# One order string and four small edits: cheaper FFT angles, an early table switch, a joined load and paired stores in a fused FFT-convolution and FFN kernel

## The chip, the cores and the metric

The kernel runs on one core of one Trainium2 chip. The metric is device microseconds (us) of one execution. Several executions of each kernel are timed beside executions of the kernel before on the same chip, and one of them is profiled. The span of a run is shorter than its device time (189.8 for 191.62). The profile of the kernel before is of a run outside the four of the comparison. Engines: PE is TensorE, ACT ScalarE, DVE VectorE, POOL GpSimd, SP the engine that issues most transfers.

## The reference, cut to what matters

```python
# x: 2048 tokens x 640, bf16; F = 1728
def reference(A_q, A_k, A_v, A_shift_k, A_ssm_k, A_ssm_D, B_x, B_w1, B_b1, B_w2, B_b2):
    x  = A_q
    xn = layernorm(x)                                  # over the 640 columns
    # long convolution:
    kv = causal_conv4(A_k, A_shift_k) * A_v            # 4 taps per column
    y  = irfft(rfft(kv, 4096) * rfft(A_ssm_k, 4096))[:2048]
    s  = xn * (y + kv * A_ssm_D)
    # FFN:
    h  = gelu(xn @ B_w1 + B_b1)
    g  = silu(h @ B_w2 + B_b2)
    return x + s * g
```

## The kernel before

The convolution is done as matrix products in two stages. The first (`s1`) multiplies by a table `W` of sines and cosines, its result is staged in SBUF, stored to DRAM and loaded again in another layout; the second (`s2`) follows, then the product of the two spectra, and the inverse (`i1`, `i2`) with a trip through DRAM between. The two FFN products (`f1` with GELU, `f2` with SiLU) are interleaved with it on PE. The columns are done in two halves, b0 and b1.

The kernel first describes every operation and what it depends on. A long string, `ORDER`, then says in which order the operations are emitted, on which engine, and in which slot of its buffer pool each result lies. That string is the schedule; 800 operations are placed by it.

```python
plan = Plan(unpack(ORDER))
...
# angles: m = tok * k4, an integer, then m mod L and (m + L/4) mod L
op("iq1", "DVE", lambda e: eng(e).tensor_single_scalar(out=m_v, in_=m_v, scalar=L - 1, op=ALU.bitwise_and), writes=[m_b],
   after=[o for o in plan.ops if o.kind == "xn"])
def iq2(e):
    eng(e).tensor_single_scalar(out=a_v, in_=m_v, scalar=L // 4, op=ALU.add)
    eng(e).tensor_single_scalar(out=a_v, in_=a_v, scalar=L - 1, op=ALU.bitwise_and)
...
sc = 2.0 * math.pi / L
op("wsin", "ACT", lambda e: nc.scalar.activation(out=W_c[:, 1, :], in_=m_v, func=ACT.Sin, scale=sc * (1.0 - EPS), bias=bias_pi[:]), ...)
op("wsin", "ACT", lambda e: nc.scalar.activation(out=W_c[:, 0, :], in_=a_v, func=ACT.Sin, scale=-sc * (1.0 - EPS), bias=bias_p[:]), ...)
...
def finish(j):                       # one row tile of 128 tokens
    op("fin", "DVE", lambda e: eng(e).tensor_tensor(out=xs(j), in0=xn[:, j, :], in1=xs(j), op=ALU.add), ...)
    op("store", "SP", lambda e: nc.sync.dma_start(out=out_v[:, j, :], in_=xs(j)), ...)
...
def conv_unit(b, u):                 # second stage of the convolution, unit u of half b
    kin, uin = Buf(pool=kin_pool, parts=nh), Buf(pool=uin_pool, parts=nh)    # four u buffers
    ...
    chain("uin", op("uin", "SP", lambda e: rd(scrU, uin), ...))              # load
    # s2k, s2u on PE, eviction in place, product on DVE, i1 on PE,
    # then the u buffer takes i1's result and is stored before it is loaded anew
```

## Time and profile before

| | before |
|---|---|
| device time, median of 4 runs of the comparison | 190.49 us (189.39 to 191.81) |
| profiled run | 191.62 us, span 189.8, mean granted PE clock 0.976 |
| busy PE / DVE / ACT | 176.4 / 164.6 / 146.5 us |
| ACT table loads | 8, of 1.28 us each |

"Slow" needs a word. On one core the label means only that the run was over 1.5% above the fastest of its kernel. I collected the 56 runs of the kernel before that accompanied four of my batches: they spread from 186.82 to 193.12 us. In 36 of them the mean clock was under 0.99, and they averaged 190.4 us; the other 20 averaged 189.5, and the 11 of these at 0.995 or more 188.9. So some dip of PE's clock comes in most runs of this kernel, not in all, and is worth some 1 to 1.5 us. The mean doesn't say where the clock fell: the profiled run has one dip, near 130 us, but the second profile that I took has two (clock 0.50 from 8 to 10 us, 0.66 from 130 to 135).

The prediction below shows the busy row, the slices, the window rows and the chain at the hole in PE's work. Two more views: the first is ACT's start (start in us, duration, engine, line, operation, what was written and read):

```profile
2.02 1.28 ACT L368 ACT_TABLE_LOAD   x1 [2.02 <-issue]
...
9.53 2.48 ACT L265 COPY xnT<-ps 128x640 bf16<-128x640 bf16 x4
12.03 1.28 ACT L456 ACT_TABLE_LOAD   x1
13.32 1.44 ACT L456 ACTIVATE W<-mm,bias_pi 128x1024 bf16<-128x1024 int32 x1
```

ACT loads a first table, evicts the first transposes, and only at 12.03 loads the table with Sin. W is there at 16. The second is what PE waited for between 28 and 80 us (who waits, for what: us in total, times, longest):

```profile
PE ps L610 <- DVE v_all L639: 0.9, 1, 0.9
PE ps L513 <- ACT sl L580: 0.5, 1, 0.5
PE ps L576 <- ACT sl L580: 0.5, 1, 0.5
PE ps L513 <- ACT hT L519: 0.2, 1, 0.2
```

Four waits, 2.1 us together: these are the "small waits" of the prediction.

### The profile page before, as it was taken

To read this page: it belongs to the slowest core of one execution; us is meant where nothing else is said; L and a number is where in the kernel's file an instruction comes from. 1 tells how busy PE (TensorE), PEld (TensorE's weight loads), DVE (VectorE), ACT (ScalarE), POOL (GpSimd) and SP (SyncE) were. 2 spreads that over 40 slices of the span, in tenths; PEclk is the share of its full clock that TensorE was granted. 3 is DMA by queue.
4 is the path that set the end of the run, shared out by engine and by line. 5 is a ranking of instruction groups with operands and counts; after the bars stand their busy time and mean duration, and the time that the engine had idled before them with its cause. 6 is when DMAs were issued, how large, how long until landed. Compare 5 with 4: busy or idle time off the path is not lost.

```text
span 189.8 us, 4770 instructions
## 1 busy us (share of the span) xinstructions
PE 176.4 (93%) x1907; PEld 92.2 (49%) x1907; DVE 164.6 (87%) x302; ACT 146.5 (77%) x225; POOL 20.6 (11%) x35
## 2 busy tenths in 40 slices
PE   7899999999898899999999999985999999989990
PEld 2285543345554465656433444332246565646660
DVE  6799979994799999999989999996498998669993
ACT  2899799797986999999999999994599987111110
POOL 4470410031021030000001100110010000000000
PEclk9999999999999999999999999996699999999997
DMA  5999969999999987898699998879762999568375
GB/s 141 350 418 414 408 200 348 323 310 379 384 333 328 234 282 206 155 293 252 137 298 286 243 380 256 240 192 327 215 207 50 342 303 337 157 214 338 107 260 191
DMA packets 44410, 51.44 MB, mean 271 GB/s; under 512 B 7442, under 2 KB 38547, under 8 KB 44388
## 3 DMA queue, kind: packets, MB, share of 16 engines
q1 hardware_dynamic: 43216, 47.03, 77.8%
q0 software_dynamic: 1024, 4.10, 6.4%
q8 instruction: 15, 0.25, 0.6%
q14 instruction: 7, 0.06, 0.1%
q10 hardware_dynamic: 148, 0.01, 0.1%
HBM read 31.47 MB, written 18.35 MB: 262 GB/s over the span
## 4 chain that ended last, share of the span: by engine, by line
PE 45%; DMA 29%; DVE 17%; ACT 4%; issue 2%; SPq 1%; POOLq 0%; ACTq 0%; DVEq 0%
PE ps L513 18%; PE ps L576 14%; DMA scrC<-v_all 9%; DMA mm<-scrC 7%; DMA kT<-in_x_dram 4%; PE ps L610 4%; DMA scrK<-mm 3%; PE ps L723 3%; DVE stats L383 3%; DMA v_all<-scrU 3%; DVE xn L784 2%; DMA x<-in_x_dram 2%; ACT mm L265 2%; DVE kT L557 2%; PE ps L777 1%
## 5 line engine op out<-in xcount | busy, mean ns | idle before, releaser
L513 PE MATMUL ps<-xnT,w_sb 128*128 128x512 bf16 (+1 forms) x280 | 64.5, 379 | 0.9 <-ACT sl L580 0.5
L576 PE MATMUL ps<-w_sb,hT 128*128 128x320 bf16 x432 | 63.6, 300 | 0.5 <-ACT sl L580 0.5
L576 PEld LDWEIGHTS <-hT 128*128 128x128 bf16 x448 | 41.8, 98 | 21.6 <-issue 5.8
L265 ACT CAST mm<-ps 128x640 bf16<-128x640 f32 (+1 forms) x62 | 39.4, 703 | 4.4 <-DMA scrK<-mm 3.3
L513 PEld LDWEIGHTS <-w_sb 128*128 128x128 bf16 x280 | 26.6, 101 | 31.4 <-issue 8.9
L265 ACT CAST v_all<-ps 128x960 bf16<-128x960 f32 (+2 forms) x38 | 33.4, 916 | 6.4 <-PE ps L723 4.1
L519 ACT ACTIVATE hT<-ps,b_f 128x512 bf16<-128x512 f32 (+1 forms) x56 | 36.9, 706 | 1.7 <-PE ps L513 1.2
L580 ACT ACTIVATE sl<-ps 128x320 bf16<-128x320 f32 x32 | 13.6, 445 | 21.1 <-PE ps L576 18.8
L784 DVE TENSOR_TENSOR xn<-ps,xn 128x640 bf16<-128x640 f32 x16 | 12.6, 817 | 3.8 <-PE ps L777 3.0
L736 DVE TENSOR_TENSOR kT<-v_all,k_all 128x960 bf16<-128x960 bf16 x16 | 9.8, 652 | 4.2 <-ACT v_all L265 4.2
L723 PEld LDWEIGHTS <-tabs 64*32 64x32 bf16 x704 | 7.6, 92 | 11.7 <-issue 7.3
L635 DVE TENSOR_TENSOR mm<-k_all,mm 128x2560 bf16<-128x2560 bf16 x8 | 11.8, 1480 | 0.1
L632 DVE TENSOR_TENSOR mm<-k_all,mm 128x2560 bf16<-128x2560 bf16 x8 | 11.8, 1478 | 0.0
L723 PE MATMUL ps<-v_all,tabs 64*32 64x240 bf16 (+1 forms) x352 | 9.0, 274 | 2.9 <-DMA v_all<-scrU 2.9
L265 DVE CAST v_all<-ps 128x960 bf16<-128x960 f32 (+1 forms) x8 | 8.6, 1070 | 2.1 <-PE ps L755 1.0
L383 DVE BATCH_NORM_STATS2 stats<-kT 128x6 f32<-128x320 bf16 x16 | 6.9, 472 | 3.8 <-DMA kT<-in_x_dram 3.8
L610 PEld LDWEIGHTS <-W 64*128 64x128 bf16 x128 | 4.5, 94 | 10.7 <-issue 8.0
L736 DVE TENSOR_TENSOR k_all<-v_all,xtra 128x960 bf16<-128x960 bf16 (+1 forms) x16 | 9.0, 609 | 0.1
L390 POOL TENSOR_TENSOR rstd<-veps,mhalf 128x4 f32<-128x4 f32 (+1 forms) x5 | 6.2, 1235 | 23.6 <-DVE veps L388 23.6
L265 ACT CAST k_all<-ps 128x960 bf16<-128x960 f32 x8 | 7.8, 977 | 0.4 <-PE ps L723 0.4
L582 DVE TENSOR_TENSOR xn<-xn,sl 128x640 bf16<-128x640 bf16 x16 | 7.7, 483 | 0.1
L265 DVE CAST k_all<-ps 128x960 bf16<-128x960 f32 x6 | 6.9, 1154 | 1.0 <-ACT v_all L265 0.8
(98 smaller groups left out, 200.7 us busy)
## 6 DMA issues: line engine op xcount, KB each, us to landing
mm<-scrC SPq DMA_DIRECT2D x8, 640.0 KB, 5.5
v_all<-scrU SPq DMA_DIRECT2D x10, 480.0 KB, 4.9
scrK<-mm SPq DMA_DIRECT2D x12, 320.0 KB, 3.8
scrU<-mm SPq DMA_DIRECT2D x12, 320.0 KB, 3.6
k_all<-scrK SPq DMA_DIRECT2D x7, 480.0 KB, 5.8
scrC<-v_all SPq DMA_DIRECT2D x7, 480.0 KB, 4.9
kT<-in_kT_dram SPq DMA_DIRECT2D x4, 640.0 KB, 10.6
v_all<-in_v_dram SPq DMA_DIRECT2D x4, 640.0 KB, 8.4
```

Of the source, the lines that this page charges most:

```text
L265: (nc.scalar.copy if e == "ACT" else nc.vector.tensor_copy)(out=out_, in_=in_)
L383: nc.vector.bn_stats(out=stats[:, j, h, :], in_=xs(j)[:, h * H:(h + 1) * H])
L513: nc.tensor.matmul(out=ps.v[:, lo * P:hi * P], lhsT=w1_sb[:, ft, t, :], rhs=xnT_b[c].v[:, t, lo * P:hi * P], start=(t == 0), stop=(t == DT ...
L519: op("gelu", "ACT", lambda e: nc.scalar.activation(out=hT_b[c].v[a:z, ft, :], in_=ps.v[a:z, :], func=ACT.Gelu_apprx_tanh, bias=b1_f[a:z, f ...
L576: nc.tensor.matmul(out=ps.v[:, 0:H], lhsT=hT_b[c].v[0:M, ft, q * P:(q + 1) * P], rhs=w[:, h * H:(h + 1) * H], start=(ft == 0), stop=(ft == ...
L580: op("silu", "ACT", lambda e, h=h, ps=ps: nc.scalar.activation(out=sl.v[:, h * H:(h + 1) * H], in_=ps.v[:, 0:H], func=ACT.Silu), reads=[ps ...
L610: nc.tensor.matmul(out=ps.v[:, h, 0:H], lhsT=W[r, j + t, :], rhs=src[r, b, j + t, :], start=True, stop=True)
L632: op("kv2", "DVE", lambda e: tt(out=kt_t, in0=win(0, 2), in1=wbc(0, 2), op=ALU.mult), reads=kb + [wb_b], writes=[kvt_b], extra=[u for b in ...
L635: op("kv2", "DVE", lambda e: tt(out=kt_t, in0=win(2, 2), in1=wbc(2, 2), op=ALU.mult), reads=kb + [wb_b], writes=[kvt_b])
L723: nc.tensor.matmul(out=ps.v[32 * g:32 * g + 32, r, i * w:(i + 1) * w], lhsT=F2[i][64 * r:64 * r + 64, :], rhs=part(src.v[64 * r:64 * r + 6 ...
L736: nc.vector.tensor_tensor(out=q[:, r], in0=uu[:, r, :, None, :].to_broadcast([P, 2, 2, w]), in1=ku[:, r, None, :, :].to_broadcast([P, 2, 2 ...
L784: nc.vector.tensor_tensor(out=xv, in0=ps.v[:, :, 0:H], in1=xv, op=ALU.mult)
```

## The change

The intent: make W sooner and more cheaply, hide the table switch where ACT idles anyway, save issues and DVE work at both ends, and find an order that suits the result. The diff, without the new `ORDER` string (all of it differs) and some bookkeeping:

```diff
+NPAIR = 12
+    op("presin", "ACT", lambda e: nc.scalar.activation(out=acs[:, CH - 1, 0:1], in_=bias_h[:], func=ACT.Silu), reads=[bias_b])
-    for q in range(CH):
+    for q in range(2):
         load_first(lambda e, q=q: nc.sync.dma_start(out=x01[:, q, :], in_=x_v[:, q, :]), 160, writes=[x_b[q]])
+    load_first(lambda e: nc.sync.dma_start(out=x01[:, 2:4, :], in_=x_v[:, 2:4, :]), 320, writes=x_b[2:4])
-    op("tabsin", "ACT", lambda e: nc.scalar.activation(out=tabs[:], in_=smq, func=ACT.Sin, ...
+    def tabsin(e):
+        nc.scalar.activation(out=acs[:, CH - 1, 1:2], in_=bias_h[:], func=ACT.Silu)
+        nc.scalar.activation(out=tabs[:], in_=smq, func=ACT.Sin, ...
-    op("iq1", ... bitwise_and with L - 1 ...)
-    def iq2(e): ... add L // 4, bitwise_and with L - 1 ...
+    op("iq1", "DVE", lambda e: nc.vector.tensor_scalar(out=m_v, in0=m_v, scalar1=19, scalar2=19, op0=ALU.logical_shift_left,
+                                                       op1=ALU.arith_shift_right), writes=[m_b])
+    op("iq2", "DVE", lambda e: nc.vector.scalar_tensor_tensor(out=a_v, in0=m_v, scalar=-1.0, in1=m_v, op0=ALU.mult, op1=ALU.min),
+       reads=[m_b], writes=[a_b])
-    ... func=ACT.Sin, scale=sc * (1.0 - EPS), bias=bias_pi[:])
+    ... func=ACT.Sin, scale=-sc * (1.0 - EPS))
-    ... func=ACT.Sin, scale=-sc * (1.0 - EPS), bias=bias_p[:])
+    ... func=ACT.Sin, scale=sc, bias=bias_h[:])
-    def finish(j):     ... one add of 640 columns and one store per tile
+    def finish(j, n):  ... for tiles 0 to 11 one add of 1280 columns and one store per pair (n == 2)
```

The two shifts leave a signed angle in [-L/2, L/2), so the sine needs no bias; the cosine is the sine of pi/2 minus the magnitude. The SiLU calls write one unused column; they exist to bring a table in.

## The prediction

> **What bounds the kernel now.** I first read the busy row and the slices of the page, then the busy times per 5 us stretch, then the chain of waits between 118 and 136 us, then the order of instructions at both ends. The span is 189.8 us (device time 190.48 us unprofiled); "us" below is trace time until the last step.
>
> ```profile
> PE 176.4 (93%) x1907; PEld 92.2 (49%) x1907; DVE 164.6 (87%) x302; ACT 146.5 (77%) x225; POOL 20.6 (11%) x35
> PE   7899999999898899999999999985999999989990
> PEclk9999999999999999999999999996699999999997
> ```
>
> PE is busy nearly everywhere: the lost time is at the left end, in slices 27 and 28, and at the right end. The busy times per stretch (PE, PEld, DVE, ACT, POOL, granted clock, DMA share, GB/s) size the hole:
>
> ```profile
> 120.00:125.00 5.00, 5.00 (x82) 2.13 (x81) 4.62 (x11) 4.81 (x7) 0.88 (x2) 1.00 0.92 264
> 125.00:130.00 5.00, 2.53 (x41) 0.89 (x38) 4.96 (x10) 3.38 (x7) 0.16 (x1) 0.94 0.89 245
> 130.00:135.00 5.00, 4.55 (x56) 1.52 (x57) 1.54 (x3) 2.52 (x3) 0.00 (x0) 0.50 1.02 287
> 135.00:140.00 5.00, 5.00 (x86) 2.00 (x92) 3.65 (x7) 4.25 (x7) 0.83 (x1) 0.88 0.71 196
> ```
>
> PE stops for about 2.5 us and then runs at half clock for about 5 us more. The chain there tells why (start, us, what):
>
> ```profile
> 117.65 1.16 DVE v_all L265
> ...
> 119.33 5.93 DMA scrC<-v_all
> ...
> 125.32 5.08 DMA v_all<-scrU
> ...
> 130.45 1.00 PE ps L723 x25
> ```
>
> One of the four u buffers of the convolution is evicted to, stored (5.93 us), then loaded anew for a later unit (5.08 us), and PE's forward matmuls of that unit wait. From the end of the producing inverse step (i1, 117.45) to the landing (130.41) the **round trip is 13.0 us**; an earlier one, stored from SP's queue, took about 10.6 (97.1 to 107.7).
>
> To see how much PE work the loss sits between, I summed PE's work in program order at its full pace: 14 matmuls of the second FFN product take 2.01 us in the chain, 5 of the first 1.19; I took 0.17 for a step of the first FFT stage, 0.27 of the second, 0.62 of the inverse. The sum is 167.3 us (an estimate; small steps are rounded). The first real transpose starts at 8.78, and the last matmul ends at 185.05, so 9.0 us are lost between: 0.5 before the first FFN product (10.88), 2.4 from there to 76 us in small waits, about **5.7 in the hole** (2.85 idle, the rest half clock), and some 0.5 at the end. After the last matmul, 4.7 us are the tail: SiLU 0.44, multiply 0.48, add 0.49, store issue, landing (about 1.9).
>
> **What the Trainium skill says.** "ScalarE: Activation LUTs", What ACT_TABLE_LOAD costs: a table load is about 1283 ns; the trace agrees, 8 loads of mean 1283 ns. "ScalarE activation tables: per-element evaluation and per-set limits", What a function is on this engine: functions of one set need no switch; before, Gelu and SiLU do switch (3 loads each), and no trace here yet shows whether SiLU and Sin share a set. "VectorE: DVE Perf Modes", Mode 2×_2P: a 4-byte op with one source may run at two elements a cycle, one with two tensors only at one; the trace agrees, 128x1024 takes 0.68 us as a one-source op and 1.23 us with two tensors (but the in-place add-and-mask pair had 0.70 and 0.97). "TensorE: Matmul & The Clock Gate", What's actually happening: an idle window of about 3.4 us halves the clock; here 2.85 us of idle was followed by a clock of 0.50.
>
> **The change part by part.**
>
> *Angles.* Three one-source ops (0.68 + 0.70 + 0.97 = 2.35 us) become one with two shifts (0.68, as the mask) and one two-tensor op (1.23): DVE saves 0.44. The Sin steps stay at 1.4 each. This is no path by itself.
>
> *Tables.* I counted switches in the new order of ACT. The dummy SiLU loads its table while ACT is idle anyway (its load now is at 2.02, followed by 2.21 us of waiting), so the Sin load at 12.03 (1.28) goes. But the small-table Sin stands among the Gelus of the first chunk, not by the first SiLU, and SiLU and Gelu alternate once more: 11 loads for 8, **+3.85 us on ACT**, plus about 0.5 for the dummies.
>
> *Stores.* Sixteen adds (0.483) become six of 1280 columns (0.82, like the other 128x1280 ops) and four single ones: 7.73 - (4.92 + 1.93) = 0.88 us saved on DVE, and 6 store issues of 0.33 to 0.5 us on SP. The last two stores stay single, so the 4.7 us tail stays; DVE backlog delays the last multiply by perhaps 0.15 now.
>
> *x load.* One issue of 0.42 us less on SP before the first weights. Tiles 2 and 3 land about 5.5 to 5.9 as now.
>
> *The order.* All instructions are in a new order, and this is the largest part. Evictions move to DVE (six more of the u stage, some fewer elsewhere: about +4.0 us by 1.15 each for the large ones), and off ACT (about -2.9). Sums: DVE 164.6 - 0.44 - 0.88 + 4.0 = **167**, ACT 146.5 + 3.85 + 0.5 - 2.9 = **148**. PE's work does not change.
>
> *Its start.* W comes sooner: first Sin about 6 to 7.4, second, behind the two sums of tile 2, about 9.5 to 11. PE then does five k steps and a transpose before the first FFN product, which needs an xn transpose that ACT evicts in 10th place: two wide-bias evictions at 0.5, a k eviction at 0.7, then it, to 13.3; the other half waits for a further transpose evicted at about 16.6. By then PE has done 4.5 us of its sum, so it runs 12.1 behind it, and with the small table's two loads some 12.6 by 30 us, where before ran 9.4 behind. **The start costs about 3 us**, some of which comes back because before loses 2.2 more until 76 us with these evictions.
>
> *Its middle.* For each reuse of a u buffer I summed PE's work from the producing i1 to the consuming step. Before: 15.3, 11.4, 12.9, **10.0** (the hole), 11.5, 13.1, 13.2, 13.7. After: **9.8**, 11.4, 16.1, 13.0, 14.3, 14.7, 14.5, 13.5. Against a trip of 10.6 to 13.0 the hole should close (13.0 of work where it was 10.0), while the first reuse (9.8) may wait 1 to 2 us. So the middle gives 5.7 and takes about 1.5.
>
> Sum of delays behind PE's work: 12.6 at 30 us, 1.0 to 76, 1.5 at the first reuse, 0.6 at the end = 15.7; PE ends at 167.3 + 15.7 = 183.0, and with the tail 187.7. Against 189.8 that is **-2.1 us**. On 190.48 us: 188.4; since the order was plainly searched for, and my start may be too pessimistic by a microsecond, I take **187.9 us**.
>
> **The rivals.**
> - *The hole moves.* The first reuse has only 9.8 us of work; if SP holds the load behind another store, PE idles near 3 us there and the clock halves as it did before. For it: the same pattern with 10.0 us. Against it: 10.6 us was enough once. It would give the 5.7 back: 190 to 192.
> - *DVE becomes the bound.* DVE was busy 9.8 to 9.9 of each 10 us from 50 to 90, and gets 2.6 us more in all. With the hole gone the same work must fit in less time, some 97% full from 10 to 155 us. Then PE waits for PSUM in many small pieces: 188.5 to 190.
> - *The start is not dearer.* If ACT and DVE keep to a better pace than my hand reckoning, or before's 2.2 us of small waits vanish altogether, only the hole counts: 184.5 to 186.
> - *SiLU and Sin share no set.* Then there are three loads more, one of them in the start: about 2 to 3 us worse than said. The dummy exists for this purpose, so I give it little.
>
> **Range and chances.** The better start gives the low end, 184.6, the moved hole or full DVE the high end, 190.8. The 2% line is at 186.7 us; that needs the hole closed and the start dear by at most 2 us: 0.33. Slower by 2% (194.3) needs two rivals at once: 0.04.
>
> **What would show it.** Right: no PE idle over 1 us at the fourth u reuse and a clock near 1.00 from 125 to 140; the first full FFN product after 12 us; 11 table loads; DVE near 167 and ACT near 148 busy; a tail near 4.7; perhaps 1 to 2 us of PE waiting for the u load near the first reuse (90 to 102 us). Wrong: a first FFN product by 11 us (start mis-sized), a clock dip elsewhere (hole moved), or many PE waits on DVE between 50 and 120.

## The result, and the profile after

The changed kernel took 184.33 us (median of 4 runs, 183.93 to 185.5) against 190.49. Ratios in this document are the mean time of one kernel's fast runs over that of the other's fast runs of the same rounds, so not quite the ratio of the medians: here 0.9684, 95% interval 0.9608 to 0.9761, faster. I had predicted 187.9 with a range of 184.6 to 190.8 and "within 2%" as the likeliest: so I had forecast too small a gain, and the result lies just under the range. Three later batches on other chips gave 183.36, 185.14 and 184.37, so the median of 20 runs is 184.35.

The page of the changed kernel; the profiled run is 183.93 us, clock 0.997:

```profile
PE 172.1 (94%) x1892; PEld 90.3 (50%) x1907; DVE 166.1 (91%) x298; ACT 149.2 (82%) x227; POOL 22.5 (12%) x37
PE   6999997999999999999999999999899999999990
PEclk9999999999999999999999999999999999999998
```

PE is busy 4.3 us less in a span 7.7 us shorter. The clock no longer falls in the middle, but the 4.3 doesn't measure that: 15 matmul records are missing from this trace, and two complete traces, the second of before with its dips and the third of after, have 173.1 and 173.3. DVE 166.1 and ACT 149.2 are the 167 and 148 of the prediction. The stretch of the hole, with the columns that the prediction explains:

```profile
120.00:125.00 5.00, 4.68 (x96) 2.26 (x97) 4.82 (x9) 4.74 (x7) 1.07 (x2) 1.00 1.09 348
125.00:130.00 5.00, 4.43 (x77) 1.69 (x76) 4.22 (x9) 4.98 (x9) 0.71 (x1) 1.00 0.63 181
130.00:135.00 5.00, 4.68 (x111) 2.80 (x103) 4.06 (x8) 4.24 (x6) 0.00 (x0) 1.00 1.08 326
135.00:140.00 5.00, 4.95 (x87) 2.67 (x73) 4.76 (x8) 4.59 (x8) 0.00 (x0) 1.00 1.01 286
```

No stretch has less than 4.43 of 5 us of PE, missing records included. The chain of waits at the same place (start, us, what):

```profile
121.83 5.55 DMA scrC<-v_all
127.45 7.07 DMA v_all<-scrU
...
134.56 0.60 PE ps L732 x32
```

The store and load of a u buffer still stand in the chain, and they are not shorter: 5.55 and 7.07 us against 5.93 and 5.08. But they are nearly hidden: PE waits for such a load twice in this trace, 0.51 us at the fourth reuse (129.68) and 0.32 at the next (134.56), where one wait alone was 2.85. ACT's start:

```profile
2.04 1.28 ACT L304 ACT_TABLE_LOAD   x1 [2.04 <-issue]
3.33 0.20 ACT L304 ACTIVATE acs<-bias_h 128x1 f32<-128x1 f32 x1
4.13 1.07 ACT L266 CAST mm<-ps 128x512 bf16<-128x512 f32 x2 [0.59 <-PE ps L481]
5.09 1.35 ACT L459 ACTIVATE W<-mm 128x1024 bf16<-128x1024 int32 x1
...
11.24 0.70 ACT L266 COPY xnT<-ps 128x640 bf16<-128x640 bf16 x1
```

No load stands ahead of the Sin at 5.09: the table that SiLU brought serves it. The first xn transpose that PE needs is evicted at 11.24 to 11.94; I had put its end at 13.3. And PE's waits between 28 and 80 us:

```profile
PE ps L501 <- DVE xn L405: 0.8, 1, 0.8
PE ps L516 <- DVE xnT L266: 0.3, 1, 0.3
PE ps L516 <- issue: 0.2, 1, 0.2
```

1.3 us instead of 2.1, and the two that have a releaser end by 30.6 us; from 31 to 80 no wait of PE for another engine or a load is listed.

To add this up I use the sum of the prediction: the **lag** is the time at which PE starts a piece of work, less the PE work (at full pace, 167.3 us in all) that stands before it in the order. A wait raises the lag by its length. The sum's small steps are a little too long, so the lag of a PE that never waits sinks slowly, by about 0.8 us from 30 to 76. The tail is the time from the last matmul to the end of the span. All values are us and come from one trace each:

| kernel | lag at 30 | 76 | 104 | 140 | end | tail |
|---|---|---|---|---|---|---|
| predicted for after | 12.6 | 13.6 | 15.1 | 15.1 | 15.7 | 4.7 |
| after | 10.9 | 10.0 | 10.3 | 9.9 | 10.5 | 4.31 |
| after, three more traces, mean | 10.3 | 9.5 | 9.7 | 9.2 | 10.3 | 4.47 |
| before | 9.8 | 11.6 | 11.7 | 16.9 | 17.7 | 4.75 |
| before, second trace | 8.2 | 10.6 | 10.7 | 15.5 | 16.6 | 4.82 |

Between the two kernels' first traces the start costs 1.1 us more, the stretch from 30 to 76 gives 2.7, the hole some 5.6, and the tail 0.4: together the 7.7 us of span. This compares a slow run of before with a fast run of after. Both traces of before have the clock dip, so the 5.6 includes it. At a full clock the hole is worth less (1.6 us in two fast runs of E4 below), and the whole change some 4.5: the eleven runs of before at a clock of 0.995 or more averaged 188.9, the median of the changed kernel is 184.35.

### The profile page after: what moved, and what is told of

It reads as the page before. It is cut to its first block, busy times and chain, and to the rows that moved or that the text cites. A ratio compares the mean times of both kernels' runs of the same rounds, so it can differ in the third digit from the quotient of the medians.

```text
span 182.1 us, 4749 instructions
## 1 busy us (share of the span) xinstructions
PE 172.1 (94%) x1892; PEld 90.3 (50%) x1907; DVE 166.1 (91%) x298; ACT 149.2 (82%) x227; POOL 22.5 (12%) x37
## 3 DMA queue, kind: packets, MB, share of 16 engines
q0 software_dynamic: 1216, 4.75, 7.7%
## 4 chain that ended last, share of the span: by engine, by line
PE 57%; DMA 17%; DVE 14%; ACT 5%; issue 3%; POOL 1%; SPq 0%; DVEq 0%; POOLq 0%
PE ps L585 25%; PE ps L516 17%; DMA v_all<-scrU 6%; PE ps L619 5%; DMA scrC<-v_all 5%; PE ps L732 5%; DVE xn L793 3%; DMA scrU<-mm 3%; ACT mm L266 3%; DMA mm<-scrC 2%; PE ps L764 2%; DVE kT L564 2%; DVE x L564 2%; PE ps L547 1%; DVE stats L386 1%
## 5 line engine op out<-in xcount | busy, mean ns | idle before, releaser
L516 PE MATMUL ps<-xnT,w_sb 128*128 128x512 bf16 (+1 forms) x265 | 60.1, 367 | 1.7 <-issue 0.9
L516 PEld LDWEIGHTS <-w_sb 128*128 128x128 bf16 x280 | 25.3, 99 | 29.2 <-issue 6.8
L266 ACT CAST v_all<-ps 128x960 bf16<-128x960 f32 (+1 forms) x33 | 29.8, 943 | 1.4 <-PE ps L732 0.8
L589 ACT ACTIVATE sl<-ps 128x320 bf16<-128x320 f32 x32 | 14.2, 446 | 20.3 <-PE ps L585 17.4
L266 DVE CAST v_all<-ps 128x960 bf16<-128x960 f32 (+2 forms) x13 | 13.7, 1053 | 2.7 <-PE ps L764 1.7
L793 DVE TENSOR_TENSOR xn<-ps,xn 128x640 bf16<-128x640 f32 x16 | 12.4, 818 | 2.1 <-PE ps L786 2.0
L266 ACT CAST k_all<-ps 128x960 bf16<-128x960 f32 x13 | 12.6, 984 | 0.8 <-PE ps L732 0.8
L624 POOL DMA_DIRECT2D scrK<-mm x7 | 5.0, 726 | 44.8 <-ACT mm L266 44.8
L745 DVE TENSOR_TENSOR k_all<-v_all,k_all 128x960 bf16<-128x960 bf16 x16 | 9.7, 653 | 0.8 <-ACT v_all L266 0.8
L393 POOL TENSOR_TENSOR rstd<-veps,mhalf 128x4 f32<-128x4 f32 (+1 forms) x5 | 7.5, 1497 | 22.6 <-DVE veps L391 22.6
L775 POOL DMA_DIRECT2D scrC<-v_all x5 | 4.1, 821 | 46.1 <-ACT v_all L266 28.8
```

The lines of the kernel that those rows point to most:

```text
L266: (nc.scalar.copy if e == "ACT" else nc.vector.tensor_copy)(out=out_, in_=in_)
L516: nc.tensor.matmul(out=ps.v[:, lo * P:hi * P], lhsT=w1_sb[:, ft, t, :], rhs=xnT_b[c].v[:, t, lo * P:hi * P], start=(t == 0), stop=(t == DT ...
L589: op("silu", "ACT", lambda e, h=h, ps=ps: nc.scalar.activation(out=sl.v[:, h * H:(h + 1) * H], in_=ps.v[:, 0:H], func=ACT.Silu), reads=[ps ...
L745: nc.vector.tensor_tensor(out=q[:, r], in0=uu[:, r, :, None, :].to_broadcast([P, 2, 2, w]), in1=ku[:, r, None, :, :].to_broadcast([P, 2, 2 ...
L793: nc.vector.tensor_tensor(out=xv, in0=ps.v[:, :, 0:H], in1=xv, op=ALU.mult)
```

## The experiments

Fifteen more runs were made, of eleven variants, of the changed kernel three times and of the kernel before once, all correct to the reference. They are named by the first part of their labels (E1 is e1_edits_old_order, A3 is a3_no_dummy_silu). Where an expectation speaks of lags, some are in a closer rounding of the same sum (164.9 us in all); differences between kernels are the same in both.

### Which half: the edits or the order?

Two kernels cross the parts. The first is the changed code with the old order (operations that exist only after put where their counterpart stood), the second the old code with the new order.

```diff
# e1_edits_old_order: after.py
-ORDER = """ ...after's... """
+ORDER = """ ...before's, with presin first and each joined operation at the place of its last part... """
# e2_new_order_old_code: before.py
-ORDER = """ ...before's... """
+ORDER = """ ...after's, with each joined operation split again... """
```

> All four named edits of the change (shifts and folded cosine, dummy SiLU before Sin, one load for x tiles 2 and 3, paired stores), but the instruction order of the kernel before. Theory (the new order made the gain, the edits are near 0 by themselves): 189 to 191 us, within 1% of before, 8 or 9 table loads, PE still idle near 3 us around 128 us with a clock dip after it. Rival (the edits made the gain by taking 1.3 us off DVE and a table load off the start): 185 to 187 us.

> The code of the kernel before (masks, no dummy SiLU, single x loads, single stores) in the instruction order of the changed kernel. Theory (order): 184.5 to 186.5 us, no PE idle over 1 us from 120 to 140 and no clock dip; a little of the start is lost, as the second Sin comes later and one or two table loads come on top. Rival (edits): 188 to 190 us.

| | old order | new order |
|---|---|---|
| old code | 189.73 (27 runs) | 187.56 (20 runs) |
| changed code | 189.85 (4 runs) | 183.36 to 185.14 (four batches) |

The first row and the lower left are medians on one chip. The ratio of the edits alone is 1.015 (1.0047 to 1.0253), yet the medians are equal: of before's 27 runs half were labelled slow and left out of the mean, while all four of the edits' runs, as long as those, were kept; the verdict on record is unclear. I read it as no change (over all runs the ratio of the means is 1.001). The order alone has 0.9939 (0.990 to 0.9978): small, 2.2 us in the medians, about 1 us in fast runs, and between the two ranges that I had expected.

So the edits alone give nothing, the order alone 1 to 2 us, both together about 6: they need each other. The lags say how. In the old order with the edits PE falls behind in the old hole as before (10.4 at 124 us, 15.2 at 140). In the new order with the old code there is no hole (11.1 and 12.0), and no small waits either (12.4 at 30, 11.5 at 76), but it starts 1.5 to 2.4 us later than the after traces, since the new order puts the first `s1` step, which needs W, at the head, and the tail is 5.25 against 4.3 to 4.5. The new order asks for W at 9.8 us; in the old one nobody needed it before 22.5. PE's wait for W says it directly: 2.09 us in E2 (to 11.23), 0.39 in after (to 9.84). E2's clock then fell too (0.55 and 0.59 in 12 to 14 and 14 to 16 us), which a dip by chance would also give. **The order takes the waits away, and the edits make the order's start affordable.**

### Is it the hole? Fill it in before, open it in after

```diff
# e3_hole_filled: before.py, ORDER only
+ two f1 steps (2.4 us of PE work) ahead of s2u b1 u1 t0, the step that waits in the hole
# e4_hole_opened: after.py, ORDER only
+ s2u b1 u1 t0 ahead of two f1 steps: 10.6 us of PE work between the i1 that fills its buffer and it, where after has 13.0
```

> The kernel before with one thing moved: two first-FFN steps (5 matmuls each, 1.19 us) stand ahead of the forward step that waited 2.85 us for its u load. Theory (the hole is a missing 3 us of work in one u reuse, and the clock dip is its consequence): PE idle there falls to about 0.5 us, the granted clock stays near 1.00, and the time falls by 4 to 6 us, to 184.5 to 186.5. If the dip has another cause, only the 2.4 us of idle go, 188 us. Rival (DVE is the bound): under 1 us.

> The changed kernel with one thing moved: the waiting forward step of the fourth u reuse stands two first-FFN steps (2.4 us) earlier, so that 10.6 us of PE work are left between the inverse step and it where there were 13.0. Theory (a reuse with less work than its round trip costs the difference, and the two steps that now come later do not fill it): PE idle of 1.5 to 2.5 us there, the time 1.5 to 2.5 us over the yardstick, more (up to 5 us) if the clock dips after it. Rival (the trip is shorter in this order, as at the first reuse where 9.8 us were enough): under 0.5 us.

Filling missed. Before with the filled hole took 189.51 (four runs, 187.79 to 190.11; ratio 1.0124, interval 0.9957 to 1.0291): no gain to be seen. Its trace (clock 0.999) shows PE's waits from 118 to 142 us:

```profile
PE ps L723 <- ACT v_all L265: 0.9, 1, 0.9
PE ps L723 <- DMA v_all<-scrU: 0.8, 1, 0.8
PE ps L755 <- ACT v_all L265: 0.5, 1, 0.5
```

The wait for the transfer fell from 2.85 to 0.8, but PE now waits for evictions by ACT that come just after it. The lag still rises from 11.1 at 124 to 13.8 at 140, that is 2.7 where before rises 5.6 with its dip. Two of the four runs had a mean clock of 0.982. One of before's holes can be filled without a microsecond to show for it. Either the work behind it was also late, or the two steps are missed where they had stood; the trace doesn't separate these.

Opening did hurt: 188.31 (186.62 to 191.69) against 185.14 for after in the same batch. The four runs fall in two groups. Two kept a full clock and took 186.62 and 186.85, 1.6 us over after. Two had a mean clock of 0.982 and 0.979, and took 191.69 and 189.78, 4.6 to 6.6 over. The profile is of the 191.69 us run; its windows:

```profile
125.00:130.00 5.00, 2.30 (x40) 0.84 (x38) 4.38 (x11) 3.93 (x7) 0.71 (x1) 0.94 0.67 215
130.00:135.00 5.00, 3.59 (x24) 1.29 (x25) 0.00 (x0) 0.69 (x1) 0.00 (x0) 0.50 1.10 328
135.00:140.00 5.00, 5.00 (x83) 2.16 (x82) 2.60 (x4) 3.61 (x5) 0.00 (x0) 0.88 0.22 65
```

This is before's hole over again, made by two steps in the wrong place: 3.6 us of waiting for the u load, then half a clock. Only the 1.6 us is seen in fast runs; the dip's further 3 to 5 us come in some executions.

### The small waits between 28 and 80 us

In before DVE stands still for 3.8 us at 44.75, waiting for a late x tile. My theory was that this stall makes DVE late and so causes the small waits; the experiment lets DVE do four steps of the k convolution first.

```diff
# e6_stats_later: before.py, ORDER only
+ stats 8, 9, 10 behind kvc..kvf of b0 i3 (those DVE steps run in the stall)
```

> The kernel before with the statistics of x tiles 8, 9 and 10 moved behind four more vector steps of the k window, so that DVE does not stand still for 3.8 us (44.75 to 48.53) for the load of these tiles. Theory (this stall is what made the kernel before fall a further 2 us behind PE's work between 28 and 62 us, where the changed kernel does not): DVE idle there under 1 us, the time falls by 1.5 to 2 us, the hole at 128 us stays. Rival (DVE has slack there): no change, within 0.5 us.

The stall went (3.8 to 0.3 us of DVE waiting for that load), and the time stayed: 189.48, ratio 0.9983 (0.9903 to 1.0063). The trace shows why this settles little. DVE got new waits, 1.9 us for POOL and 1.2 for ACT, so that it waits 3.4 us between 28 and 80 where it waited 3.8. And ACT waits there for its staging buffers, in before (first line) as in E6 (the others):

```profile
ACT mm L265 <- DMA scrK<-mm: 3.3, 3, 1.2
ACT mm L265 <- DMA scrK<-mm: 2.2, 2, 1.4
ACT mm L265 <- DMA scrU<-mm: 1.6, 1, 1.6
```

ACT waits until a staging buffer has been stored, and in E6 PE waits for these evictions in turn (1.2 us). The theory is not confirmed, nor quite refuted: this one stall can go without a gain, but DVE was hardly relieved in sum. What does remove the small waits is the new order as a whole: they are gone in the old code with the new order, and they stand in the changed code with the old order (1.8 us: 0.8, 0.5, 0.3 and 0.2). ACT's waits for staging stores go with them: 3.3, 3.8, 2.0 and 3.8 us in before, its second trace, E1 and E6, none in after and E2. That makes these waits the suspect, but no run isolates them or any single move; more staging buffers, the direct test, were not run (by my count they don't fit into SBUF).

### The edits one by one, in the new order

Each edit is undone singly in the changed kernel, with the changed kernel beside it on the same chip: stores, tables and angles in one batch, the angles again and the x load in another.

> The changed kernel unaltered, as the yardstick of this chip for the three runs that undo one edit each in its order. Every theory: 184 to 185.5 us, PE lag behind its work of 10.5 to 11.5 us from 30 to 130 us, no clock dip in the middle.

After came out at 183.36 us (183.1 to 184.06), below what I expected.

```diff
# a1_single_stores
-NPAIR = 12
+NPAIR = 0
```

> The changed kernel with 16 single adds and stores in place of 6 paired and 4 single ones, all else and the order kept. The first four runs left 2.5 to 3 us to the edits inside the new order. If the stores carry it at the end (DVE backlog and six more store issues on SP after the last matmuls): 1 to 1.5 us slower, tail after the last matmul 5 us or more where it was 4.3. Rival (start carries it all): under 0.4 us slower.

184.97 us (184.18 to 186.04): 1.6 more. The lag is like that of after to 104 us (9.6 against 9.4) and then rises: 9.7 against 8.6 at 140, 11.7 against 9.6 at the end; the tail is 5.22 against 4.41. PE's waits from 100 us on, first in a1, then in after of the same batch:

```profile
PE ps L786 <- DMA mm<-scrC: 1.9, 1, 1.9
PE ps L732 <- DMA v_all<-scrU: 1.3, 2, 1.0
```

```profile
PE ps L786 <- DMA mm<-scrC: 0.8, 1, 0.8
PE ps L732 <- DMA v_all<-scrU: 0.3, 1, 0.3
```

The chain of both ends in an unbroken row of DVE steps from about 165 us on. There DVE is the bound, so its saved adds count (the row is 0.4 us longer in a1), and the tail, which I had left at 4.7, is 0.8 shorter with pairs. The other part, loads landing about 1 us later, sits in one trace of each kernel, and I cannot say how much of it is scatter.

```diff
# a3_no_dummy_silu
-    op("presin", "ACT", ... func=ACT.Silu ...)
-        nc.scalar.activation(out=acs[:, CH - 1, 1:2], in_=bias_h[:], func=ACT.Silu)
```

> The changed kernel without the two dummy SiLUs, order kept. Theory: the first Sin then needs a table load of its own behind the first evictions, and the sums of tile 2 between the two Sins may need no or two more loads: 1.3 to 2.6 us later W, first FFN product at 13.7 us or later where it was 12.45, 1 to 2 us slower. Rival: the start has slack or the compiler picks a set with Sin at once, then the time is the same within 0.4 us and the page shows 11 table loads or fewer.

186.40 us (185.57 to 186.89): 3.0 more, the largest effect of a single edit. ACT's start without them:

```profile
2.04 1.28 ACT L266 ACT_TABLE_LOAD   x1 [2.04 <-issue]
...
5.05 1.28 ACT L457 ACT_TABLE_LOAD   x1
6.35 1.35 ACT L457 ACTIVATE W<-mm 128x1024 bf16<-128x1024 int32 x1
...
12.48 0.70 ACT L266 COPY xnT<-ps 128x640 bf16<-128x640 bf16 x1
```

The first load brings some table that doesn't serve the Sin, and Sin must load its own: it starts at 6.35 instead of 5.01 in after of the same batch, the transpose is evicted at 12.48 instead of 11.17, the lag at 30 us is 12.0 against 10.0, and at the end 12.4 against 9.6. Nothing in the middle gives a late start back: what W loses at 5 us is still lost at 180. That is more than the 1.28 us of the load, and PE's start shows where the rest comes from (A3, then after of the same batch):

```profile
11.07 0.72 PE L617 MATMUL ps<-kT,W 64*128 64x320 bf16 x4 [1.80 <-ACT W L459]
13.69 1.27 PE L514 MATMUL ps<-xnT,w_sb 128*128 128x256 bf16 x5
```

```profile
9.77 0.72 PE L619 MATMUL ps<-kT,W 64*128 64x320 bf16 x4 [0.40 <-ACT W L461]
11.94 0.71 PE L516 MATMUL ps<-xnT,w_sb 128*128 128x256 bf16 x5
```

PE waits for W and starts 1.30 us later. Then the same five matmuls take 1.27 us instead of 0.71, and the long run of f1 behind them starts 2.58 us later (17.03 against 14.45). So half of the loss is the load, the other half PE at about half pace until 17 us. The windows print a clock of 1.00 there, but the packed trace has no clock record before 17.15 us in A3 (11.31 in after), so this 1.00 is not a measurement. The slow pace also comes unasked: in the first trace of the unchanged kernel those five matmuls take 1.27 us too, and the lag at 30 us is 10.9 there, against 10.0 where they take 0.71. All four runs of A3 are above all four of after, so the sum of 3.0 stands (I had expected 1 to 2), but how much of it is the pace by chance is not shown.

```diff
# a2_mask_angles (and a2b: the same, its constant in a spare column of acs, so that no buffer moves)
-    iq1, iq2: two shifts; minimum of m and -m
+    iq1, iq2: mask; add, mask        # three DVE passes, with the biases of before
```

> The changed kernel with the angle operations of before (mask, add, mask, and a bias for both Sins), order kept. DVE gets 0.45 to 1 us more between 3 and 8 us, ahead of the statistics and of xn 0 and 1, so the first k step and the first transposes come later by that: 0.4 to 1.0 us slower if the start is on the path (theory); 0 to 0.2 if the start waits for loads anyway (rival).

> The changed kernel once more, unchanged, as the yardstick of the next two on their chip. From its three earlier medians (184.33, 183.36, 185.14) about 184.3 us; its spread from chip to chip is 1.8 us, so the two kernels beside it are judged against this run and not against those.

> The changed kernel with the masked angles of before (three DVE passes in place of two), this time without a new tile: the one constant lies in a spare column of the accumulators, so every buffer keeps its address. In the earlier run of this undoing the start was unchanged and 1.8 us came at the very end, where no angle is made. Theory one, the angles are worth the 0.7 us of one DVE pass at most and the 1.8 was scatter of the last transfers or of the addresses: within 0.7 us of the yardstick, PE's lag at 28 us within 0.5 us of it. Theory two, the angles are worth 1.8 us: 1.5 to 2 us over the yardstick.

The first undoing took 185.18 (184.24 to 185.35), 1.8 over its yardstick, but its trace has the start of after (lag 10.1 against 10.0 at 30, 8.6 at 140 for both), and all of the difference near the end (10.8 against 9.6), where no angle is made. So I ran it again with unmoved buffers and a new yardstick: 185.32 (184.47 to 185.56) against 184.37 (183.72 to 185.72), 0.95 over. This time the trace is later from the start: 11.2 against 10.0 at 30, 0.3 of which is already there when the first wide-bias matmul starts (2.62 against 2.30 us, a landing time). The rest can be PE's pace again: the first five f1 matmuls took 1.27 us against 0.71, as in the first trace of the unchanged kernel, whose lag of 10.9 is nearly this one. The add-and-mask pair took two passes of 0.69 in it, 1.38, where the single two-tensor pass takes 1.22; the DVE work differs by only 0.16. Neither theory of the expectation fits (0.7 us at most, or 1.5 to 2). The angles are worth perhaps 1 us; the traces don't agree on where, and the intervals overlap (0.9693 to 0.9809 of before against 0.9658 to 0.9776). The sure part is small: the Sin without a bias takes 1.35 us, those with one 1.42 to 1.46.

```diff
# a4_x_loads_split
-    for q in range(2): ...        # and one load for tiles 2 and 3
+    for q in range(CH): ...
```

> The changed kernel with the third and fourth tile of x in two loads, as before, in the same place of the order. Theory one, the start is set by the tables and the wide bias, not by these tiles: within 0.5 us of the yardstick. Theory two, one issue less on the queue brings the weights and the K rows about 0.6 us earlier (an issue takes about that long on the queue that issues it): 0.5 to 1 us slower than the yardstick, with PE's lag at 14 us larger by as much.

184.43 us (183.2 to 186.15) against 184.37: nothing. Theory one holds; the joined load has no part in the result.

### The small tables among the GELUs

The order after puts the small-table Sin in the midst of GELUs, which costs ACT two extra switches. Here it is moved to the first SiLU.

```diff
# e5_tabs_by_silu: after.py, ORDER only
+ tabsin, tabscale right before the first f2 and SiLU
```

> The changed kernel again, as the yardstick on the chip of the next two. 183 to 185.5 us.

> The changed kernel with the small-table Sin moved from among the Gelus at 23 us to directly ahead of the first SiLU, as the change's words say: two table loads fewer (9 for 11), 2.6 us less on ACT between 23 and 27 us. Theory (PE is the bound and PSUM depth hides ACT there): the same within 0.5 us, PE lag at 30 us unchanged. Rival (ACT holds PE at 28 to 32 us, where PE waited 0.84 us): 0.5 to 1 us faster.

After took 185.14 (183.7 to 188.44), this one 185.18 (183.49 to 186.73). It has 9 table loads for 11 and ACT is busy 147.0 us for 149.2, and none of it shows in the time: loads in ACT's middle lie beside other work.

> The kernel before once more, for a second trace: its runs on one chip lay between 186.8 and 192.5 us. Theory: the hole (PE idle 2 to 3 us near 128 us) is in every run, and what differs is whether the clock dips after it (mean clock 0.975 to 0.98 with a dip, 0.995 and over without): about 187 to 188 us without, 190 to 191.5 with it. Rival: the spread has other places.

The extra profile of before (190.64 us, span 188.7, clock 0.981) serves as the second trace in the table of lags. Its hole: 2.63 us of PE in 125 to 130 at a full clock, then 4.77 at 0.66. It idled 2.5 us, and the clock fell for a shorter time than in the first profile. One more run can't say whether the hole is in every run; and its clock of 0.981 is the sum of two dips (one before 11 us), so my expectation's reading of the mean clock, dip behind the hole or none, was too simple.

No variant beat the changed kernel.

## Why the prediction was wrong

By its own sum: 12.6 + 1.0 + 1.5 + 0.6 = 15.7 of lag, and a tail of 4.7. Measured in the profiled run: 10.5 and 4.31, 5.6 us less. Three terms failed: the start was mis-sized, and two waits that I charged, 1.0 us of small waits and 1.5 at the first reuse, did not come. The mechanism of the hole was right.

**"The start costs about 3 us" failed.** The predicted lag at 30 us was 12.6, the measured 10.9 (and 10.3 in the mean of three more traces). Against before's 9.8 that is a cost of 1.1, not 2.8 (between the later traces, 10.3 against 8.2, it is 2.1: one to two us, not three). I began ACT's queue one microsecond too late: the first wide-bias matmul ran at 2.44 in this profile, where in before it stands behind six warm-up matmuls at 3.92 (I had reckoned with 3.3). Sin ran at 5.09 and 8.36 where I said "about 6" and "about 9.5", and every eviction behind it moved up with it: 11.94 for 13.3, and the other half of the transpose, whose eviction starts at 14.43, for 16.6. 1.7 us of the miss. The sign that I had named for a mis-sized start, a first FFN product by 11 us, did not show it: that product came at 12.45, "after 12" as for a right prediction.

**"1.0 to 76" failed.** I charged the new order with some of before's small waits. Past 31 us there are none: the lag sinks from 10.9 to 10.0. E2 shows that the order does this also with the old code. 1.9 us of the miss, of which 0.8 is the rounding of the sum that lets every lag sink. The prediction had named this in its third rival ("before's 2.2 us of small waits vanish altogether", 184.5 to 186), and gave it too little weight in the chances.

**"1.5 at the first reuse" failed: that wait did not come.** i1 ends at 88.60 and the step starts at 98.61, straight behind the matmul before it; the trace lists no wait of PE for a u load from 84 to 106 us. So the trip took 10.0 us at most: the store, issued at 89.99, landed in 3.6 us (5.93 in before's hole), and the load was issued at 93.66. The lag rose by 0.3 from 76 to 104, 1.2 us of the miss. I had read the trip as 10.6 to 13.0 from two cases of before; it is not a constant.

**The hole: right.** The lag falls from 10.3 to 9.9 over the stretch, the clock stays at 1.00, and the fourth reuse, with 13.0 us of work, nearly covers a trip of 12.9 (i1's end at 116.85 to the landing at 129.7): PE waits 0.51 us. The margin is thin: in E5's trace the same step waited 1.52 us, with the clock at 1.00. E4 confirms it from the other side: with 10.6 us of work the hole is back. What the prediction did not see is that the hole's worth differs from run to run, since the dip comes in some runs only; and E3 shows that in the old order filling it alone gives nothing.

**Tables, stores, x load.** 11 loads came as counted, but E5 shows that those in the middle are free, so that only where they stood mattered. SiLU and Sin share a set, so the fourth rival did not come, and A3 prices the early switch at 3.0 us. The tail came out 0.4 shorter, not longer: I had let the last DVE backlog add 0.15, but the paired adds relieve the very stretch where DVE is the bound (A1: 0.8 us of tail). The x load's saved issue is worth nothing (A4).

**Two rivals did not come.** DVE as a bound: its busy time between 50 and 90 is 39.45 of 40 us, against 39.48 before, and PE did 39.79 us of work in it where before did 38.57. There DVE is full but doesn't make PE wait, so it is not the bound in that stretch. The moved hole: no dip in the profile, and 19 of the 20 runs of the changed kernel had mean clocks of 0.994 or more; the one at 0.991 was the longest, 188.44 us, and has no trace.

One thing in the arithmetic remains: the traced span 187.7 would have meant 189.5 us of device time, and I subtracted the difference from the median instead, since before's profiled run was a slow one. That helped by a microsecond, by luck and not by insight; without it the miss would have been larger.

**Still open**: which moves of the order take away the small waits, what the angles are worth apart from PE's pace before 17 us, what sets that pace in each run, and how much of A1's later loads is scatter.

## What to carry to other kernels

Sum the bounding engine's work in program order and follow its lag: a wait counts only where the lag rises and does not sink again. A late start passed to the end in full here (A3), and an extra table load in the middle cost nothing (E5), so the same 1.28 us costs its whole length and more at one place and nothing at another. An edit can be worth nothing in one order and decide in another (all the edits together gave nothing in E1, the early switch alone 3 us in A3): test it in the schedule that needs it, and give a searched order the credit of having removed small waits that you can't assign.

## What the Trainium skill lacked or had wrong

- "ScalarE: Activation LUTs", What ACT_TABLE_LOAD costs: it states about 1283 ns for the load and about 1380 ns of drain, 2.66 us for a switch. The load agrees (1283 ns in every profile). The drain doesn't show: in A3 the load stands at 5.05 to 6.33 and the Sin starts at 6.35, and before it the casts end at 5.03. A switch on a busy ACT costs 1.3 us here.
- "ScalarE activation tables: per-element evaluation and per-set limits", What a function is on this engine, says that functions of one set need no switch; the pages don't say that SiLU and Sin share one. They do: after the SiLU at 3.33 us the Sin at 5.09 needs no load.
- "TensorE: Matmul & The Clock Gate", What's actually happening: it gives an idle window of about 3.4 us, free-running, before the clock halves. That the dip comes in some runs of a kernel and not in others agrees (2 of 4 runs of E4; 36 of 56 runs of before had a mean clock under 0.99). But the idle gaps of the holes were 2.85 and 2.5 us in the two profiles of before, less than a window, and in the first the clock fell inside the gap (0.70 in 129 to 130, PE idle since 127.6). In the five profiles with a gap of 2.5 us or more in the middle (before twice, E1, E4, E6) the clock fell to 0.50; gaps of 1.85 us (A1, at 164.6) and 1.52 (E5, at 130.2) left it at 1.00. So in these traces 2.5 us of idle was already too long.
